# A shorter work share in every second long period of an attention and SwiGLU kernel's instruction order

## The chip, the core and the metric

The kernel runs on one core of a Trainium2 chip. The metric is the device time of one execution in microseconds. The core has five engines that run side by side, each through its own instructions in order: TensorE (PE; its weight loads, PEld, overlap its matmuls), VectorE (DVE), ScalarE (ACT), GpSimd (POOL) and SyncE (SP), whose queue issues most DMAs. They wait for one another through semaphores. Matmuls write PSUM banks, from which VectorE and ScalarE read.

## What is computed

`x` is 2048 × 512. One half of the kernel is softmax attention with 32 heads of 16, the other a SwiGLU block with 1792 inner columns; a gate per token mixes them.

```python
def _A_ref(x, wqkv, wo):
    ...
    scores = jnp.einsum("bhqd,bhkd->bhqk", q, k) * scale
    p = _softmax(scores, axis=-1)
    o = jnp.einsum("bhqk,bhkd->bhqd", p, v)
    return (lambda x, *d: x.transpose(*d))(o, 0, 2, 1, 3).reshape(B, S, D) @ wo

def _B_ref(x, w1, w3, w2):
    gate = jnp.einsum("bsd,df->bsf", x, w1)
    up = jnp.einsum("bsd,df->bsf", x, w3)
    h = _silu(gate) * up
    out = jnp.einsum("bsf,fd->bsd", h, w2)
    return out

g = _sigmoid((x * gate_w).sum(-1, keepdims=True))
return g * a + (1 - g) * b
```

## The kernel before

A prologue transposes and splits x, projects V and the first 128 columns of Q and K, and writes Q and K to device memory. Matrix products outside attention are made of three products of a high and a low half of each operand (fh, fl for weights, xH, xL for x; the names xH and xL are used again later for the halves of w2 and of the attention output).

Then one long loop, about 1280 us, mixes two streams on TensorE. Its order is a string, `order`, one letter per piece of TensorE work:

- **Q**: a unit of scores. There are 1024 units, 32 for each of 32 steps (a pair of heads and half of the queries). A unit is two matmuls, side by side in the two 64-row halves of the array, into a buffer S of two PSUM banks; there are two such buffers. ScalarE then takes the exp of the unit into one of eight buffers p (L795).
- **P**: the weighted sums with V (called PV below) of the two oldest units, four matmuls over the full array into `acc` (L779). After the sixteenth key tile `evac` copies `acc` to `u` on VectorE and stores it (L766, L773).
- **F**: a work slot. Each slot issues up to one matmul in each of two lanes, the two 64-row halves of the array, from a list of blocks: the remaining Q and K columns, gate and up products in chunks of 128 columns (L432), the products of h with w2 (L550), the first part of the output projection (L636, L643). A block of `length` slots runs first in one lane and then, at least GAP later, in the other; when both are done VectorE (and ScalarE) take it from its bank. The matmul of the second half waits for a small VectorE memset, `tick` (L752).

A period is eight Q with its F and P. In `one`, the long period, it is two scores and six slots, then a score and three slots five times, one last score and four P in a row. In `two`, the double, it is fifteen slots, and the four P stand in two groups of two with two scores between. The first part of the loop is long periods, the second doubles; the joint between them begins with `QQFFF`.

Other work is hung on the letters. At every Q, one or more items of `small` (pieces of the gate's sigmoid on VectorE), `loads` (loads of w2 rows and of pieces of h, each with a split into halves on GpSimd, L513 and L514) and `stages` (division by the softmax sums) are issued. `load_step` issues the Q and K rows of the next step, fourteen DMAs, when the count of units is 6 modulo 32. Weight splits (L328, L329) are issued a fixed number of units after their load. `load_w2` is added to `loads` when the last up block of a column block is done, so it follows the F stream; a step's loads follow the Q stream. SP takes all these DMAs in the order in which they are issued.

After the loop, `while feed()` empties the lanes, and the rest of the output projection is done with full-array matmuls (L96 to L98).

Of the kernel before, what the change touches and what calls it, by code (L numbers as in the profile page):

```python
# [33 lines left out]
def gated_mix_kernel(ctx: ExitStack, tc: tile.TileContext, x, wqkv, wo, w1, w3, w2, gate_w, out):  # L34
# [765 lines left out]


    NP = 8
    LONG, SHORT = 77, 51
    one = "QQFFFFFF" + "QFFF" * 5 + "QPPPP"
    two = "QFFF" * 5 + "QPPQQPP"
    order = one * LONG + "QQFFF" + two * (SHORT - 1) + "QFFF" * 4 + "QFQPPPP"
    free = list(range(NP))

    units = iter([(j, half, k, gq) for half in range(2) for j in range(NPAIR) for k in range(NT) for gq in range(2)])
# [112 lines left out]
```

## Time and profile before

| | us |
|---|---|
| median of 3 runs | 1403.82 |
| the three runs | 1403.82, 1403.74, 1717.74 |
| profiled execution, time | 1402.91 |
| profiled execution, span | 1401.1 |

The span runs from the first to the last instruction of the profiled execution; its time is 1.8 us longer. The granted TensorE clock is 1.000 over the span. In the rows below, a timeline row is: start, duration, engine, line, operation, output <- inputs, count of equal instructions merged, and in brackets the idle time before and what ended it. A row of the chain is: start, duration, engine, tile, line. A row of a group is: line, engine, operation, count, then busy time and the mean ns of one, then the idle time before. Ends of matmuls are modelled, so starts are compared. A TensorE row of 0.39 us whose successor starts 0.23 later is an overlapped pair.

### The profile page before, as it was taken

Reading aid. Unit: us, or ns where it says so; the run is one execution under the profiler, and the core shown is the slowest. Engines: PE = TensorE matmul, PEld = TensorE weight load, DVE = VectorE, ACT = ScalarE, POOL = GpSimd, SP = SyncE. Lnnn points to the kernel's source line nnn. Section 1 sums busy time; section 2 is a strip of 40 time slices with the busy share of each in tenths; the row PEclk is TensorE's granted clock in tenths of the full one; section 3 lists DMA queues with packets and bytes.
Section 4 is the critical chain, followed back from the end, with each engine's and each line's share of the span. In section 5 each row is a group of like instructions: output and inputs, shape, how many; then the busy total and the mean of one; then the engine's idle time right before and its main releaser. Section 6 shows DMA issues by size and latency. Waiting matters only on the chain.

```text
span 1401.1 us, 28802 instructions
## 1 busy us (share of the span) xinstructions
PE 1394.2 (100%) x11398; PEld 819.8 (59%) x11398; DVE 486.6 (35%) x1069; ACT 1032.8 (74%) x1153; POOL 321.1 (23%) x357
## 2 busy tenths in 40 slices
PE   9999999999999999999999999999999999999998
PEld 8866566565565565565565565555555555555556
DVE  5511111564545556555464654411111111110013
ACT  4457677777777777777777777788778878877880
POOL 6123433011011101110110117241233232133240
PEclk9999999999999999999999999999999999999999
DMA  7753564343223423223332236444443433355445
GB/s 205 174 121 97 135 135 112 74 112 77 50 54 84 114 55 84 62 67 96 69 77 70 78 80 169 97 99 98 106 96 89 109 102 81 63 127 116 89 136 178
DMA packets 112814, 141.44 MB, mean 101 GB/s; under 512 B 16416, under 2 KB 70944, under 8 KB 109600
## 3 DMA queue, kind: packets, MB, share of 16 engines
q1 hardware_dynamic: 110240, 135.32, 40.8%
q10 hardware_dynamic: 2432, 4.20, 0.9%
q8 instruction: 92, 1.51, 0.5%
q14 instruction: 50, 0.41, 0.1%
HBM read 90.70 MB, written 48.76 MB: 100 GB/s over the span
## 4 chain that ended last, share of the span: by engine, by line
PE 99%; ACT 0%; DVE 0%; issue 0%; DVEq 0%; ACTq 0%
PE acc L779 33%; PE f L432 27%; PE S L791 19%; PE f L550 11%; PE S L199 2%; PE f L96 1%; PE f L98 1%; PE f L97 1%; PE f L636 1%; ACT p L795 0%; PE acc L353 0%; PE f L165 0%; PE S L98 0%; PE S L97 0%; PE S L96 0%; PE S L165 0%
## 5 line engine op out<-in xcount | busy, mean ns | idle before, releaser
L795 ACT ACTIVATE p<-S 128x1024 f32<-128x1024 f32 x1024 | 967.4, 1026 | 298.9 <-PE S L791 289.7
L779 PE MATMUL acc<-p,V 128*17 128x512 f32 x4096 | 474.1, 594 | 0.0
L791 PE MATMUL S<-Qt,Kt 50*128 50x512 f32 x2048 | 402.7, 408 | 1.2 <-DVE V L415 0.7
L791 PEld LDWEIGHTS S<-Qt,Kt 50*128 50x128 f32 x2048 | 183.1, 184 | 186.3 <-ACT p L795 85.7
L779 PEld LDWEIGHTS acc<-p,V 128*17 128x17 f32 x4096 | 102.2, 97 | 272.2 <-issue 272.2
L463 DVE RECIPROCAL sg<-sg 128x64 f32<-128x64 f32 x448 | 209.1, 517 | 49.3 <-issue 47.3
L432 PE MATMUL f<-xL,fh 64*128 64x512 f32 x1088 | 218.0, 392 | 0.0
L432 PE MATMUL f<-xH,fl 64*128 64x512 f32 x1088 | 218.0, 392 | 0.0
L432 PE MATMUL f<-xH,fh 64*128 64x512 f32 x1088 | 217.1, 390 | 0.0
L432 PEld LDWEIGHTS f<-xH,fl 64*128 64x128 f32 x1088 | 104.9, 186 | 24.0 <-POOL fl L329 0.4
L432 PEld LDWEIGHTS f<-xL,fh 64*128 64x128 f32 x1088 | 105.1, 186 | 22.4
L432 PEld LDWEIGHTS f<-xH,fh 64*128 64x128 f32 x1088 | 104.3, 185 | 23.4
L752 DVE MEMSET tick<- 1x1 f32 x189 | 11.2, 59 | 272.8 <-PE f L550 155.0
L328 POOL CAST fh<-fr 128x512 fp32r<-128x512 f32 x34 | 21.6, 637 | 357.2 <-DMA fr<-in_B_w_dram 233.4
L455 DVE COPY gs<-f 128x512 f32<-128x512 f32 x56 | 38.7, 691 | 69.0 <-PE f L432 62.8
L550 PE MATMUL f<-xL,fh 64*128 64x512 f32 x208 | 61.8, 390 | 0.0
L550 PE MATMUL f<-xH,fl 64*128 64x512 f32 x208 | 60.8, 390 | 0.0
L550 PE MATMUL f<-xH,fh 64*128 64x512 f32 x208 | 59.9, 390 | 0.0
L550 PE MATMUL f<-xH,raw 64*128 64x512 f32 x192 | 57.4, 390 | 0.0
L461 DVE TENSOR_SCALAR sg<-sg 128x512 f32<-128x512 f32 x56 | 27.2, 485 | 81.7 <-ACT sg L460 79.6
L619 POOL TENSOR_TENSOR hx<-hx,gw 128x512 f32<-128x512 f32 x8 | 10.3, 1288 | 197.3 <-DMA gw<-r_d 186.7
L760 DVE COPY u<-acc 128x512 f32<-128x512 f32 x32 | 22.1, 692 | 96.1 <-PE acc L779 81.7
(230 smaller groups left out, 1281.4 us busy)
## 6 DMA issues: line engine op xcount, KB each, us to landing
Kt<-kH_d SPq DMA_DIRECT2D x128, 128.0 KB
h_d<-sg SPq DMA_DIRECT2D x56, 256.0 KB
sg<-h_d SPq DMA_DIRECT2D x43, 256.0 KB
fr<-in_B_w_dram SPq DMA_DIRECT2D x42, 256.0 KB
Qt<-qH_d SPq DMA_DIRECT2D x128, 64.0 KB
Kt<-kL_d SPq DMA_DIRECT2D x64, 128.0 KB
Qt<-qL_d SPq DMA_DIRECT2D x64, 64.0 KB
b_d<-y SPq DMA_DIRECT2D x16, 256.0 KB
```

What stands on the lines that cost most here:

```text
L96: nc.tensor.matmul(ps, sH, mH, start=first, stop=False)
L199: nc.tensor.matmul(ps[:, i, :], w[i][h][:, k, :], xs[b][:, k, :], start=n == 0, stop=n == len(order) - 1)
L328: nc.gpsimd.tensor_copy(hi, src)
L432: return nc.tensor.matmul(ps, w[i == 1][r, k, :], (xL if i == 2 else xH)[b][r, k, :], start=n == 0 and not second, stop=n == 3 * ND - 1 an ...
L455: nc.vector.tensor_copy(gs, ps)
L461: small.append(lambda: nc.vector.tensor_scalar(sg, sg, 1.0, None, op0=OP.add))
L463: small.append(lambda q=q: nc.vector.reciprocal(sg[:, q:q + 64], sg[:, q:q + 64]))
L550: ins = nc.tensor.matmul(ps, hs[t][q][i == 1][r, P * o:P * o + P], (w2L if i == 2 else w2H)[q][r, o, :], start=n == 0 and not second, stop ...
L760: nc.vector.tensor_copy(u, acc)
L779: nc.tensor.matmul(acc[r:r + DH + 1, :], V[:, k, 2 * j + h, :], p[:, h, :], start=k == 0, stop=k == NT - 1)
L791: nc.tensor.matmul(ps[:, h, :], Kt[i][r:r + 50, P * k:P * k + P], Qt[i][r:r + 50, t:t + 512], start=True, stop=True)
L795: nc.scalar.activation(p, ps, AF.Exp, scale=SCALE)
```

## The change

The long part had 77 periods `one`. It now has 37 pairs of `one` and `less`, and then nine more `one`, 83 periods in all. `less` is `one` with five slots instead of six between the second and the third score. The joint has four slots instead of three, and of the doubles 45 are left instead of 51 (the last one is written out with a different end).

```diff
-    LONG, SHORT = 77, 51
+    LONG, MID, SHORT = 37, 9, 45
     one = "QQFFFFFF" + "QFFF" * 5 + "QPPPP"
+    less = "QQFFFFF" + "QFFF" * 5 + "QPPPP"
     two = "QFFF" * 5 + "QPPQQPP"
-    order = one * LONG + "QQFFF" + two * (SHORT - 1) + "QFFF" * 4 + "QFQPPPP"
+    order = (one + less) * LONG + one * MID + "QQFFFF" + two * (SHORT - 1) + "QFFF" * 4 + "QFQPPPP"
```

Slots before: 77 × 21 + 3 + 50 × 15 + 13 = 2383. Slots after: 37 × 41 + 9 × 21 + 4 + 44 × 15 + 13 = 2383. Scores, PV and blocks are the same in number.

TensorE's order, second period, one piece of the difference (f is a bank of the work, S a score buffer):

```order
 L432 MATMUL f<-xL_158,fh_652 128x512
 L432 MATMUL f<-xL_158,fh_646 128x512
+L791 MATMUL S<-Qt_108,Kt_111 128x512 x2
 L432 MATMUL f<-xH_157,fh_652 128x512
 L432 MATMUL f<-xH_157,fh_646 128x512
-L791 MATMUL S<-Qt_108,Kt_111 128x512 x2
 L432 MATMUL f<-xH_157,fl_653 128x512
```

The third score of the period stands one slot (two matmuls) earlier.

SP's order where the work goes over from gate and up to the h products, before (`fr<-in_B_w` of 128x512 are rows of w2, `sg<-h_d` pieces of h, `d_d<-u` and `o_d<-u` the stores of `evac`, Qt, Kt and `m_d` the operands of a step):

```order
L512 DMA fr<-in_B_w_dram 128x512 x2
L512 DMA sg<-h_d 128x4x128
L482 DMA h_d<-sg 128x512
L512 DMA sg<-h_d 128x4x128 x2
L512 DMA sg<-h_d 128x2x128
L766 DMA d_d<-u 1x512 x4
L773 DMA o_d<-u 16x512 x4
L277 DMA Qt_109<-qH_d 16x1024
```

SP's order behind the same `evac`, at the same step, after the change:

```order
L512 DMA fr<-in_B_w_dram 128x512
L277 DMA Qt_109<-qH_d 16x1024
L277 DMA Qt_109<-qL_d 16x1024
L277 DMA Qt_109<-qH_d 16x1024 x2
L277 DMA Qt_109<-qL_d 16x1024
L277 DMA Qt_109<-qH_d 16x1024
L270 DMA Kt_112<-kH_d 16x2048 x2
L270 DMA Kt_112<-kL_d 16x2048
L270 DMA Kt_112<-kH_d 16x2048 x2
L270 DMA Kt_112<-kL_d 16x2048
L282 DMA Qt_109<-m_d 2x1024 x2
L512 DMA fr<-in_B_w_dram 128x512
```

The last two row blocks of w2 were ahead of the stores and of the step; now one is between them and the last is behind the step.

TensorE's order at the end of the loop, before:

```order
L779 MATMUL acc<-p_20915,V 17x512 x2
L779 MATMUL acc<-p_20925,V 17x512 x2
L779 MATMUL acc<-p_20930,V 17x512 x2
L96 MATMUL f<-xH_15791,raw 128x512
L97 MATMUL f<-xL_15792,raw 128x512
L98 MATMUL f<-xH_15791,raw 128x512
```

And after the change (`L643` is the last block of the output projection's first part, the one that is split between the lanes):

```order
L779 MATMUL acc<-p_20917,V 17x512 x2
L779 MATMUL acc<-p_20923,V 17x512 x2
L643 MATMUL f<-wo_19904,fl_20358 128x512
L643 MATMUL f<-wo_19904,fh_20357 128x512
L643 MATMUL f<-wo_17915,fh_20357 128x512
L643 MATMUL f<-wo_17915,fl_20358 128x512
L643 MATMUL f<-wo_17915,fh_20357 128x512
L96 MATMUL f<-xH_15867,raw 128x512
L97 MATMUL f<-xL_15868,raw 128x512
L98 MATMUL f<-xH_15867,raw 128x512
```

Five matmuls of that block now stand behind the last P, ahead of the tail. Within the loop 2370 slots hold two matmuls, 12 hold one and one is empty before; 2364 hold two and 19 hold one after.

## Prediction

> **What bounds the kernel now.** I read the busy times first, then the chain that ended last, then the timeline of single periods.
>
> ```profile
> PE 1394.2 (100%) x11398; PEld 819.8 (59%) x11398; DVE 486.6 (35%) x1069; ACT 1032.8 (74%) x1153; POOL 321.1 (23%) x357
> PE 99%; ACT 0%; DVE 0%; issue 0%; DVEq 0%; ACTq 0%
> L795 ACT ACTIVATE p<-S 128x1024 f32<-128x1024 f32 x1024 | 967.4, 1026 | 298.9 <-PE S L791 289.7
> L779 PE MATMUL acc<-p,V 128*17 128x512 f32 x4096 | 474.1, 594 | 0.0
> ```
>
> TensorE is never free and the chain is 99% TensorE, so a change that only reorders pays or gains through two things: extra TensorE time at switches, and TensorE waiting. ScalarE is the second busiest, and its idle time ends on scores (S), so it is the first engine TensorE could come to wait for. The chain gives the long period, by the starts of its weighted sums (PV, written acc, L779):
>
> ```profile
> 87.31 3.56 PE acc L779 x32
> 286.75 3.56 PE acc L779 x32
> 297.23 3.56 PE acc L779 x32
> 874.58 3.56 PE acc L779 x32
> ```
>
> From 87.31 to 874.58 lie 75 long periods: 787.27 / 75 = 10.497 us. Most take 10.50, some 10.48 (286.75 to 297.23). The doubles, from the timeline of TensorE, where a block of PV is half as long:
>
> ```profile
> 904.71 1.91 PE L779 MATMUL acc<-p,V 128*17 128x512 f32 x16
> 914.13 1.91 PE L779 MATMUL acc<-p,V 128*17 128x512 f32 x16
> 1102.46 1.91 PE L779 MATMUL acc<-p,V 128*17 128x512 f32 x16
> ```
>
> 914.13 to 1102.46 is 20 doubles of 9.417 us. A long period has 21 work slots and a double 15, with the same scores and PV. The timeline of one long period shows a slot's price and who is close behind:
>
> ```profile
> 300.71 0.73 PE L791 MATMUL S<-Qt,Kt 50*128 50x512 f32 x4
> 301.32 7.54 ACT L795 ACTIVATE p<-S 128x1024 f32<-128x1024 f32 x8 [2.45 <-PE S L791]
> 302.45 0.19 PEld L791 LDWEIGHTS S<-Qt,Kt 50*128 50x128 f32 x2
> 302.69 0.39 PE L791 MATMUL S<-Qt,Kt 50*128 50x512 f32 x2
> 302.92 0.40 PE L432 MATMUL f<-xH,fl 64*128 64x512 f32 x2
> 305.25 0.39 PE L432 MATMUL f<-xH,fh 64*128 64x512 f32 x2
> 307.65 3.63 PE L779 MATMUL acc<-p,V 128*17 128x512 f32 x32
> ```
>
> Starts on TensorE are 0.23 apart, so a slot costs 0.23 us. From the first two scores (300.71) to PV is 6.94. The third score reuses the S buffer that the first exp reads. That exp starts at 301.32 and, with the mean of 1.026, ends at 302.35; the score's weight load goes at 302.45. So only about 0.10 is free there, less than the slot that is taken out.
>
> **The change part by part.**
>
> *Six doubles become long periods.* Per pair 10.497 − 9.417 = 1.08, so 6 × 1.08 = +6.5 us. The six extra long periods bring 36 slots, and the joint between the two parts one more.
>
> *The joint.* It is `QQFFF` before and `QQFFFF` after. Its rows are also the best evidence for the next step:
>
> ```profile
> 888.57 0.73 PE L791 MATMUL S<-Qt,Kt 50*128 50x512 f32 x4
> 889.17 7.44 ACT L795 ACTIVATE p<-S 128x1024 f32<-128x1024 f32 x8 [2.45 <-PE S L791]
> 890.25 0.50 PE L791 MATMUL S<-Qt,Kt 50*128 50x512 f32 x2 [0.25 <-ACT p L795]
> 895.31 1.91 PE L779 MATMUL acc<-p,V 128*17 128x512 f32 x16
> ```
>
> With three slots ahead of the third score TensorE waits for the exp (0.25 shown), so a fourth slot there is hidden: 0. If the exp came earlier it would cost 0.23.
>
> *Thirty-seven periods lose a slot, 21 to 20.* The joint is such a period with two slots fewer still: three F stand before its third score where the short period has five, and all else up to PV is alike. From 888.57 to 895.31 is 6.74, against 6.94. Three slots (0.70) were taken out and 0.20 came back; the rest went into the wait for the exp. A short period, with one slot out (0.23), can't come below this floor, so it saves 0.20, or 0.18 where the long one took 10.48. Bounds: 0 (the wait eats the slot) and 0.23 (nothing waits). I take 0.19, near the joint's row: 37 × 0.19 = −7.0 us. The exps keep up: eight take 7.44 at the joint, (7.44 − 1.03)/7 = 0.92 or a little less each, against 0.93 for a score and its three slots.
>
> The Trainium skill ("ScalarE: Activation LUTs", section "What ACT_TABLE_LOAD costs") gives an activation with immediate scale and bias as 186 ns + 0.833 ns per element with 93 ns overlap, an estimate of 0.946 us per exp here. By that ScalarE would be slower than the scores and most of the slot would turn into waiting, a sum of about +7.7 (the slow rival below). The rows above, under 0.92 where the exps set the pace, are shorter; I go by them.
>
> *The stall at 820.9 goes.*
>
> ```profile
> 819.20 1.65 POOL L329 TENSOR_TENSOR fl<-fr,fh 128x512 fp32r<-128x512 f32 x1
> 820.51 0.39 PE L791 MATMUL S<-Qt,Kt 50*128 50x512 f32 x2
> 820.90 0.50 PE L432 MATMUL f<-xH,fl 64*128 64x512 f32 x2
> 821.23 0.39 PE L432 MATMUL f<-xL,fh 64*128 64x512 f32 x2
> ```
>
> The last chunk's weights were split (819.20 + 1.65 = 820.85) just when TensorE needed them: 820.90 instead of 820.74, and the next pair 0.33 behind it instead of 0.23, so 0.25 in all. After the change the work lags the scores by some 35 slots here, so the same split, which follows the scores, is several microseconds early: −0.25 (bounds −0.25 and 0). Nothing is late next there: the scores are paced as elsewhere.
>
> *Five matmuls spill past the end.* Slots are 2383 in both orders, but in the new one the two lanes fall out of step more often (19 slots of one matmul, against 12 and an empty one), and five matmuls of the last o_half block, one lane, come after the last PV.
>
> ```profile
> 1364.09 0.39 PE L643 MATMUL f<-wo,fh 64*128 64x512 f32 x1
> 1364.32 0.39 PE L643 MATMUL f<-wo,fl 64*128 64x512 f32 x1
> 1365.42 0.50 PE L791 MATMUL S<-Qt,Kt 50*128 50x512 f32 x2 [0.25 <-ACT p L795]
> 1388.44 0.69 DVE L886 TENSOR_TENSOR p<-fr,p 128x512 fp32r<-128x512 f32 x1 [0.78 <-ACT p L885]
> 1391.43 0.39 PE L96 MATMUL S<-wo,p 128*128 128x512 f32 x1
> ```
>
> One lane alone also takes 0.23 per matmul, so 5 × 0.23 = +1.15 us. TensorE carries the tail: its last operand is ready at 1389.13 and used at 1391.43, so that 2.3 hides nothing of the five. The last period's slots, fuller than before, cost 0, since the last score waits 0.25 for its exp in any case; without that cover +0.23. Lower bound of the spill 0, if the tail waited for data.
>
> *A load falls behind a step's operands.* The loads of w2 follow the work, load_step follows the scores. The work is now some 20 slots later there, so w2's last row block, which stood ahead of the evacuation and load_step, stands behind step 21's fourteen DMAs on SP's queue (Qt, Kt and m_d). Nothing on TensorE waits for those DMAs soon, but the h product of token tile 0 needs that row block. Prices, SP and GpSimd (POOL):
>
> ```profile
> 878.14 0.66 PE S L791 x4
> 878.92 1.12 SPq L766 DMA_DIRECT2D d_d<-u  x4
> 881.88 0.37 SPq L512 DMA_DIRECT2D fr<-in_B_w_dram  x1
> 884.62 0.61 POOL L513 CAST xH<-fr 128x512 fp32r<-128x512 f32 x1 [4.41 <-DMA fr<-in_B_w_dram]
> 885.32 1.29 POOL L514 TENSOR_TENSOR xL<-fr,xH 128x512 fp32r<-128x512 f32 x1
> 922.98 0.36 SPq L277 DMA_DIRECT2D Qt<-qH_d  x1
> 929.15 1.12 SPq L512 DMA_DIRECT2D sg<-h_d  x2
> 935.02 0.61 POOL L513 CAST fh<-sg 128x512 fp32r<-128x512 f32 x1 [12.09 <-DMA sg<-h_d]
> ```
>
> Let T be the first scores of the period that begins with unit 640 (878.14 is such a place). The stores start at T + 0.8 and the first w2 load goes at T + 3.7, as in these rows. The fourteen DMAs take 929.15 − 922.98 = 6.2, so the last w2 load goes near T + 10.4. A w2 load alone reaches GpSimd 2.7 later (881.88 to 884.62); a load right behind a step's fourteen, 5.9 later (929.15 to 935.02). The split adds 0.61 + 1.29 and a gap, 2.0. So the low half is ready between T + 15.1 and T + 18.3. TensorE wants it in the next period at the third slot after the fifth score: T + 10.5 + (305.25 − 300.71) = T + 15.0. The wait is 0.1 to 3.3; I take 2.2, nearer the load behind a step, because Kt's bytes have to drain first, but w2's rows are longer pieces than h_d's. No other work covers it: TensorE runs in order.
>
> *Sum:* 6.5 + 0 − 7.0 − 0.25 + 1.15 + 2.2 = +2.6. The profiled execution took 1402.91 (span 1401.1), so 1405.5; the median shown, 1403.82, lies 0.9 higher, so I give 1406.4.
>
> **The rivals.**
>
> *Forecast, 0.64:* as summed. With the w2 wait from 0.1 to 3.3 and the saving from 0.17 to 0.21 per short period, 1403.5 to 1408.3.
>
> *The load lands in time, 0.16:* w2's rows pass the Kt rows and the wait is 0. Then +0.4, 1404.2. For it: 2.7 alone. Against it: 5.9 behind a step. The Trainium skill ("DMA: Bandwidth & Descriptors", section "Anatomy of one DMA — SWDGE (gpsimd) path") fits 2.0 us plus the bytes at 436 GB/s, an estimate of 2.6 for 256 KB, for another issue path; it agrees with the load alone and says nothing against the backlog.
>
> *Nothing waits, faster, 0.06:* each short period saves the full 0.23 (−8.5) and the load is in time: 6.5 − 8.5 − 0.25 + 1.15 = −1.1, 1402.7. Against it: the 0.10 that is free, and the joint.
>
> *ScalarE sets the pace of short periods, slower, 0.11:* the last score of a period waits for the sixth exp, which hangs on the five exps before it at p each. At the joint p was 0.92 and PV came at 6.74; with a slower p it comes at 6.74 + 5 × (p − 0.92). At p = 0.95 that is 6.89, so a short period saves 0.05, 37 × 0.05 = 1.9, and the change is 6.5 − 1.9 − 0.25 + 1.15 + 2.2 = +7.7, 1411.5. It decides as soon as p passes the 0.93 that TensorE gives a score and its three slots. For it: the eight exps from 301.32 took 0.93 each. Against it: there they waited on scores; at the joint, where a score waited on an exp, they were faster.
>
> *Some other block finds its operand late, 0.03:* as at 820.90, but for microseconds; 2.5 to 9 more than the forecast, 1409 to 1415.
>
> **How the numbers follow.** The predicted time is the forecast's, 1406.4. The forecast's range and the second case (0.80 together) lie within 1403.0 to 1409.0, which also leaves a little for uneven long and double periods (10.48 to 10.50 and 9.41 to 9.42, some ±0.5 us in all). A gain or loss of 2%, about what a measurement of this kernel can tell from no change, is 28 us. The slow rival would need 0.76 lost in each of the 37 short periods to reach it, and the fast one has no source for 28. So faster 0.01, same 0.97, slower 0.02, the latter two for what none of these cases names.
>
> **What would show it.** Right: short periods of 10.28 to 10.31 us, third scores in them marked as waiting for ACT p L795 by a few hundredths to 0.2; 83 long-type starts, then doubles of 9.41; no gap of 0.15 at the last chunk's first slot; five L643 rows after the last PV; one gap of 0.1 to 3.3 us on TensorE ahead of L550, released by POOL xL L514, in the second period after unit 640. Wrong: short periods at 10.27 (nothing waits) or 10.45 to 10.50 (ScalarE paces); no gap at L550, or gaps at other blocks; a gap between PV and the tail's first matmuls.

## The result, and the profile after

| | us |
|---|---|
| median of 5 runs, after | 1419.09 (1417.5 to 1421.79) |
| median before | 1403.82 |
| ratio after / before | 1.011, 95% interval 1.0099 to 1.0121 |
| profiled execution, time / span | 1418.07 / 1416.2 |

The one execution of the kernel before that took 1717.74 us was in a slower state and is left out of the ratio.

The changed kernel is 1.1% slower: +15.3 us, where +2.6 was forecast; its 1419.09 lies beyond 1409.0, the end of the forecast's range.

From the page of the changed kernel: its busy times, its chain by engine, and three groups (last in a row stands the idle time just before them and what ended it):

```profile
PE 1401.6 (99%) x11398; PEld 822.7 (58%) x11398; DVE 483.8 (34%) x1069; ACT 1028.5 (73%) x1153; POOL 319.5 (23%) x357
...
PE 92%; issue 4%; POOL 2%; DMA 1%; SPq 1%; DVE 1%; DVEq 0%; POOLq 0%
...
L432 PE MATMUL f<-xH,fh 64*128 64x512 f32 x1088 | 222.6, 392 | 3.3 <-DVE tick L752 3.3
L432 PE MATMUL f<-xH,fl 64*128 64x512 f32 x1088 | 223.2, 392 | 2.2 <-DVE tick L752 2.2
...
L550 PE MATMUL f<-xH,fh 64*128 64x512 f32 x208 | 70.6, 391 | 2.0 <-POOL xH L513 2.0
```

The chain was 99% TensorE and is now 92%; SP, POOL and DMA have come into it. TensorE waits 3.3 + 2.2 us for ticks, the small memset of L752 that lets the second half of a block write the bank, and 2.0 us for the split of w2 at L513. The busy time of TensorE has grown by 7.4 us with the same 11398 matmuls, so it seems to have run slower somewhere, too.

Where the time went is read from the starts of the periods. I count them from 0, each from the weight load of its first score to the next such load. The changed kernel's timeline, weight loads of TensorE, period 5:

```profile
133.25 0.30 PEld L791 LDWEIGHTS S<-Qt,Kt 50*128 50x128 f32 x4 [0.85 <-issue]
...
147.74 0.30 PEld L791 LDWEIGHTS S<-Qt,Kt 50*128 50x128 f32 x4 [0.85 <-issue]
```

That is 14.49 us, where the other short periods take 10.33 (median of 37). Period 12, a long one, takes 13.86 instead of 10.49, period 81, long too, 15.16, and period 72 takes 10.97. These four hold 4.16 + 3.36 + 4.66 + 0.48 = 12.7 of the span's 15.1 us. The rest: +6.5 for six doubles that became long periods, −6.0 for the short periods, −0.3 for the stall that is gone, +1.4 in the tail, +0.8 ahead of the first score.

**Period 5.** The changed kernel's timeline (start, duration, engine, line, operation): SP's queue, DVE, then TensorE.

```profile
132.46 0.57 SPq L282 DMA_DIRECT2D Qt<-m_d  x2
133.86 0.34 SPq L187 DMA_DIRECT2D qL_d<-gs  x1
...
140.60 0.69 DVE L443 COPY gs<-f 128x512 f32<-128x512 f32 x1 [4.67 <-DMA qL_d<-gs]
141.23 0.06 DVE L752 MEMSET tick<- 1x1 f32 x1
...
138.77 0.39 PE L791 MATMUL S<-Qt,Kt 50*128 50x512 f32 x2
141.35 0.50 PE L432 MATMUL f<-xH,fl 64*128 64x512 f32 x2 [2.19 <-DVE tick L752]
...
142.49 5.32 PE L779 MATMUL acc<-p,V 128*17 128x512 f32 x32
```

A finished Q/K block is copied into a `gs` tile (L443), split, and stored (L187). There are two such tiles. The stores of an earlier block now stand on SP behind the fourteen DMAs of step 2 (the last two of them are the row at 132.46). The store of 133.86 lands only at 140.5, by the last update of its semaphore, so the next copy waits 4.67 us for its tile, and the tick behind it in DVE's order waits with it. TensorE's start comes 2.58 us after the one before it instead of 0.23. When this store was issued, the last four of the step's Kt loads, 128 KB each by the page's list of DMA issues, had not landed (they land from 134.8 to 137.9), nor had the 256 KB store ahead of it (139.1). In steps_late, an experiment below in which the step's DMAs go later, the same store lands 3.4 us after its issue and not 6.6.

**Period 12** has the same wait, and other DMAs stand ahead of the stores, the evacuation's d_d and o_d (changed kernel, timeline of SP, DVE and TensorE):

```profile
212.18 1.69 SPq L773 DMA_DIRECT2D o_d<-u  x4
213.97 1.51 SPq L187 DMA_DIRECT2D qH_d<-sg  x1
215.58 0.38 SPq L187 DMA_DIRECT2D qL_d<-gs  x1
...
219.03 0.69 DVE L443 COPY gs<-f 128x512 f32<-128x512 f32 x1 [5.49 <-DMA qL_d<-gs]
...
219.78 0.50 PE L432 MATMUL f<-xH,fh 64*128 64x512 f32 x2 [3.08 <-DVE tick L752]
```

In the kernel before, the stores of two more blocks went ahead of this evacuation (202.22 to 205.49, the evacuation from 207.15); now all stand behind it, and three blocks follow one another on the two tiles. No run moved these stores alone, so how much of the delay is the evacuation's and how much the closer blocks' stays open.

**Period 81** is the place that the prediction named (changed kernel, timeline of SP, POOL and TensorE):

```profile
934.11 0.36 SPq L512 DMA_DIRECT2D fr<-in_B_w_dram  x1
...
939.33 1.27 POOL L514 TENSOR_TENSOR xL<-fr,xH 128x512 fp32r<-128x512 f32 x1
...
939.31 0.49 PE L550 MATMUL f<-xH,fh 64*128 64x512 f32 x1 [1.98 <-POOL xH L513]
...
940.66 0.49 PE L550 MATMUL f<-xL,fh 64*128 64x512 f32 x1 [0.62 <-POOL xL L514]
```

The waits are 2.0 and 0.6, but the period lost 4.7; and in period 5 the PV that follows the wait takes 5.25 us to the next score (142.49 to 147.74) instead of 3.56. The windows of the changed kernel (stretch and its length, busy time and count of PE, PEld, DVE, ACT, POOL, then the granted TensorE clock, the DMA share and GB/s) show why:

```profile
130.40:141.40 11.00, 8.81 (x78) 4.92 (x70) 1.38 (x3) 7.02 (x8) 3.61 (x5) 1.00 0.94 172
141.40:147.70 6.30, 6.30 (x40) 1.77 (x40) 0.00 (x0) 1.02 (x1) 1.85 (x2) 0.73 0.55 166
...
219.80:227.00 7.20, 7.20 (x62) 3.38 (x64) 0.06 (x1) 3.41 (x4) 1.88 (x2) 1.00 0.71 172
...
940.00:952.00 12.00, 11.38 (x86) 6.57 (x86) 0.18 (x3) 6.19 (x7) 9.20 (x12) 0.86 0.31 89
```

After the waits of periods 5 and 81 the clock was halved for 3.41 us (0.5 × 3.41 / 6.3 = 0.27 missing in the second row, 0.5 × 3.41 / 12 = 0.14 in the last), which costs half of that, 1.7 us. After the longer wait of period 12 it was not. So there are two things to test: that the order on SP makes the waits, and what makes the clock fall.

### The profile page after: what moved, and what is told of

It is laid out like the page before. It is cut to its first block, busy times and chain, and to the rows that moved or that the text cites. A ratio compares the mean times of both kernels' runs of the same rounds, so it can differ in the third digit from the quotient of the medians.

```text
span 1416.2 us, 28801 instructions
## 1 busy us (share of the span) xinstructions
PE 1401.6 (99%) x11398; PEld 822.7 (58%) x11398; DVE 483.8 (34%) x1069; ACT 1028.5 (73%) x1153; POOL 319.5 (23%) x357
## 4 chain that ended last, share of the span: by engine, by line
PE 92%; issue 4%; POOL 2%; DMA 1%; SPq 1%; DVE 1%; DVEq 0%; POOLq 0%
PE acc L779 30%; PE f L432 24%; PE S L791 18%; PE f L550 11%; PE S L199 2%; PE f L96 1%; PE f L98 1%; PE f L97 1%; PE f L636 1%; POOL gs L445 1%; POOL sg L444 0%; DMA qH_d<-sg 0%; PE f L165 0%; SPq L277 0%; DMA fr<-in_B_w_dram 0%
## 5 line engine op out<-in xcount | busy, mean ns | idle before, releaser
L791 PE MATMUL S<-Qt,Kt 50*128 50x512 f32 x2048 | 411.5, 411 | 0.8 <-DVE V L415 0.7
L432 PE MATMUL f<-xH,fh 64*128 64x512 f32 x1088 | 222.6, 392 | 3.3 <-DVE tick L752 3.3
L432 PE MATMUL f<-xH,fl 64*128 64x512 f32 x1088 | 223.2, 392 | 2.2 <-DVE tick L752 2.2
L432 PE MATMUL f<-xL,fh 64*128 64x512 f32 x1088 | 222.6, 391 | 0.0
L432 PEld LDWEIGHTS f<-xH,fh 64*128 64x128 f32 x1088 | 109.1, 185 | 23.1 <-DVE tick L752 3.5
L432 PEld LDWEIGHTS f<-xH,fl 64*128 64x128 f32 x1088 | 109.6, 186 | 21.7 <-DVE tick L752 2.6
L432 PEld LDWEIGHTS f<-xL,fh 64*128 64x128 f32 x1088 | 109.2, 185 | 19.2
L752 DVE MEMSET tick<- 1x1 f32 x189 | 11.2, 59 | 272.5 <-PE f L550 153.1
L550 PE MATMUL f<-xH,fl 64*128 64x512 f32 x208 | 74.1, 390 | 0.0
L550 PE MATMUL f<-xL,fh 64*128 64x512 f32 x208 | 72.0, 391 | 0.6 <-POOL xL L514 0.6
L550 PE MATMUL f<-xH,fh 64*128 64x512 f32 x208 | 70.6, 391 | 2.0 <-POOL xH L513 2.0
L550 PE MATMUL f<-xH,raw 64*128 64x512 f32 x192 | 59.3, 391 | 0.0
```

The source lines that it names most:

```text
L432: return nc.tensor.matmul(ps, w[i == 1][r, k, :], (xL if i == 2 else xH)[b][r, k, :], start=n == 0 and not second, stop=n == 3 * ND - 1 an ...
L550: ins = nc.tensor.matmul(ps, hs[t][q][i == 1][r, P * o:P * o + P], (w2L if i == 2 else w2H)[q][r, o, :], start=n == 0 and not second, stop ...
L791: nc.tensor.matmul(ps[:, h, :], Kt[i][r:r + 50, P * k:P * k + P], Qt[i][r:r + 50, t:t + 512], start=True, stop=True)
```

## The experiments

All times stand beside the kernel before on the same chip: 1403.9 us for the first four, 1403.54 for the last three.

**steps_late: two steps later on SP**

```diff
-            if issued % 32 == 6 and step < 2 * NPAIR:
+            if issued % 32 == (12 if step in (2, 21) else 6) and step < 2 * NPAIR:
```

> The changed kernel, but the loads of steps 2 and 21 go to SP's queue six units later (issued % 32 == 12 for these two, 6 for the others), so that in period 5 the Q/K stores of L187 and in period 81 the last row of w2 stand ahead of the step's 14 DMAs again. Nothing else is moved, and period 12, where the stores stand behind the evacuation's, stays as it is. Theory (the time was lost to blocks that found their operand late because their DMA stood behind a step's on SP): periods 5 and 81 fall from 14.49 and 15.16 to the 10.33 of their kind, both halved stretches of the clock go with them, period 12 stays at 13.9; 1419.1 - 4.2 - 4.6 = 1410.3 us (1409 to 1411.5). Rival A (the clock falls because the stream of work is denser now, and the waits lie elsewhere): a halved stretch of 3.4 us is still somewhere, 1412 to 1414. Rival B (the transfers are late through their own load on the DMA engines, wherever the step stands): 1417 to 1420.

1411.92 us (1408.63 to 1412.27), ratio 1.0053 [1.0036, 1.007]: just above the theory's range and below rival A's, so the traces decide. In the trace of steps_late the stores of period 5 go ahead of the step again, and of TensorE's groups one wait for a tick is left (timeline of SP, then the group):

```profile
132.47 0.34 SPq L187 DMA_DIRECT2D qL_d<-gs  x1
...
140.67 0.38 SPq L277 DMA_DIRECT2D Qt<-qH_d  x1
```

```profile
L432 PE MATMUL f<-xH,fh 64*128 64x512 f32 x1088 | 222.9, 393 | 3.2 <-DVE tick L752 3.2
```

Periods 5 and 81 take 10.33 and 10.49, as the others of their kind (81 and 12 are long ones; the 10.33 expected of them was a slip). Rival B falls. But period 12, untouched, took 16.68 instead of 13.86: its wait is 2.96 now, and the clock was at half for 6.83 us behind it. Rival A had a fall of the clock left over, but for another reason: here the wait is one that the changed kernel has at the same place, and it halved the clock in this execution and not in that one. One of the four runs took 1408.63 at a mean clock of 0.999, the others 1411.74 to 1412.27 at 0.997.

**lo_raw: a third buffer for the stores**

```diff
-            lo = slot("gs", F32)
+            lo = slot("raw", F32)
```

> The changed kernel, but the low half of a Q/K block lies in a tile named raw, which has three buffers, and no longer in one named gs, which has two. The order on SP is untouched: in period 5 the stores still stand behind the step, in period 12 behind the evacuation's. Theory (the DVE copy of L443 waits for a buffer whose store has not landed, and the tick that TensorE needs stands behind that copy in DVE's order): with a third buffer the copy and the tick are in time, periods 5 and 12 fall from 14.49 and 13.86 to 10.33, with period 5's halved clock; period 81 stays at 15.2; 1419.1 - 4.2 - 3.4 = 1411.5 us (1410.5 to 1413). Rival (the wait only goes on to the next tile in the row, the high half sg with its two buffers, by way of POOL's queue, and from there to a later operand): less than half of it goes, 1416 to 1419.

1410.15 us (1409.84 to 1412.45), ratio 1.0047 [1.0031, 1.0064], a little below the theory's range. The stores still stand behind the step; periods 5 and 12 take 10.33 and 10.48. TensorE's groups in lo_raw's trace keep only the wait of period 81, and the copy in period 5 now waits for TensorE, not for a store (timeline of DVE):

```profile
L432 PE MATMUL f<-xH,fh 64*128 64x512 f32 x1088 | 222.8, 392 | 0.2 <-DVE tick L752 0.2
...
L550 PE MATMUL f<-xH,fh 64*128 64x512 f32 x208 | 70.6, 391 | 3.0 <-POOL xH L513 3.0
```

```profile
137.35 0.69 DVE L443 COPY raw<-f 128x512 f32<-128x512 f32 x1 [1.25 <-PE f L432]
```

So the path from late store to tile to copy to tick is shown: the order on SP was taken away in steps_late, the shortage of tiles here, and the last link, from copy to tick, stands in DVE's rows of period 5. The profiled execution's period 81 took 16.16 us, with 2.97 of wait and a halved stretch.

**both_mended: both edits**

> Both edits together: steps 2 and 21 six units later, and the low half in raw. Theory: periods 5, 12 and 81 all stand at 10.33, no stretch of halved clock is left before the end, and what remains of the change is the rest of the forecast's sum: 1419.1 - 4.2 - 3.4 - 4.6 = 1406.9 us (1405.5 to 1408), that is 3 us above the kernel before, of which 1.4 lie behind the last PV and 0.8 ahead of the first score. Rival (37 short periods cost in other places than the three, or the clock falls all the same): above 1409.

1406.37 us (1405.69 to 1407.24, ten runs), ratio 1.002 [1.001, 1.0029], as the theory had it. Periods 5, 12 and 81 take 10.34, 10.50 and 10.49. The chain of both_mended's page and its largest wait among L432 and L550:

```profile
PE 99%; DVE 0%; DMA 0%; ACT 0%; issue 0%; DVEq 0%
```

```profile
L432 PE MATMUL f<-xH,fh 64*128 64x512 f32 x1088 | 222.4, 392 | 0.2 <-DVE tick L752 0.2
```

The clock is at full through the whole span: its next fall is recorded at 1404.21, behind the last instruction (the span is 1404.0). Some 12.7 of the 15.3 us (1419.09 − 1406.37) are thus the three places. Against the kernel before, 2.5 us are left.

**before_early: the same wait put into the kernel before**

```diff
-            if issued % 32 == 6 and step < 2 * NPAIR:
+            if issued % 32 == (4 if step in (2, 21) else 6) and step < 2 * NPAIR:
```

> The kernel before with nothing of the change, but the load of step 2 goes to SP's queue two units earlier (issued % 32 == 4 for steps 2 and 21; step 21 has no load near it here), so that the Q/K stores of period 5 stand behind the step's 14 DMAs, as in the changed kernel. Theory (the order on SP alone makes the wait): period 5 rises from 10.50 to about 14.5, with a tick that comes 2 us late and a halved stretch of the clock behind it; 1403.8 + 4.0 = 1407.8 us, or 1406.0 if the wait comes and the clock stays. Rival (it needs the short periods, which leave less time between two blocks): period 5 stays at 10.5, 1403.8 us.

1407.8 us (1406.64 to 1408.87), ratio 1.0031 [1.0019, 1.0042]. In its trace the step's DMAs go from 126.27, ahead of the stores (timeline of SP, DVE and TensorE, and the window behind the wait):

```profile
133.24 0.34 SPq L187 DMA_DIRECT2D qL_d<-gs  x1
...
140.36 0.69 DVE L443 COPY gs<-f 128x512 f32<-128x512 f32 x1 [5.24 <-DMA qL_d<-gs]
...
141.10 0.50 PE L432 MATMUL f<-xH,fl 64*128 64x512 f32 x2 [3.04 <-DVE tick L752]
```

```profile
141.60:145.00 3.40, 3.40 (x20) 1.86 (x20) 0.06 (x1) 1.42 (x2) 1.40 (x2) 0.50 0.47 156
```

Two units of difference in when one step is issued, with no short period anywhere, cost 3.9 us by the medians; in the profiled execution period 5 took 15.34 instead of 10.50. The kernel before was that close to it.

**stalls: what a wait does to the clock**

```diff
-    REST, GAP = 9, 6
+    REST, GAP = 9, 6
+    DOSE = {20 + 5 * i: 12 + 2 * (3 * i % 7) for i in range(21)}
...
                     turn = nc.vector.memset(tick[:, 0:1], 0.0)
                     after(turn, ins)
+                    for _ in range(DOSE.get(t["id"], 0)):
+                        turn = nc.vector.memset(tick, 0.0)
```

> The kernel before with waits of measured length put in: behind the tick of 21 of its blocks, five blocks apart, DVE clears a row of 128 numbers 12 to 24 times, and the second half's first matmul waits for the last of them, so that TensorE stands still for some 0 to 4 us at places where no step's load and no evacuation is due. What is counted is the halved stretches of the clock behind them. Theory, from the records of the changed kernel and of steps_late, lo_raw and before_early: the clock goes by stretches of 3.41 us that follow one another without a gap from its first rise on, and a stretch in which TensorE was idle for about half (1.7 us or more) is followed by one at half speed, which costs up to 1.7 us beyond the wait. So no idle time under 1.7 us halves it, one between 1.7 and 3.4 us does or does not by how it lies across two stretches, and one above 3.5 us always does. Rival A: only a whole idle stretch of 3.4 us halves it (then nothing below 3.4 us does). Rival B: the halving belongs to the transfers of a step or of an evacuation nearby, and not to the idle time (then none of these waits, far from both, halves it). The time itself tells nothing: 1403.9 us plus the waits and 1.7 us for each halved stretch.

One execution, 1455.81 us. Twelve of the 21 places gave a wait of 0.8 us or more; at the other nine it was hidden. The granted clock first rises at 5.59 us of the span, and every later change in its records is a whole number of 3.413 us behind that, so the span can be laid out in stretches of that length. The idle time of TensorE is taken from the modelled end of the last matmul ahead to the start of the next:

```
idle from-to, us    total  in each stretch it touches  clock behind it
201.57-202.38       0.81   0.81                        full
235.07-237.59       2.52   2.52                        half for 3.41
331.13-334.84       3.71   2.14, 1.57                  half for 6.83
370.12-371.42       1.30   0.70, 0.60                  full
394.87-397.65       2.78   2.78                        half for 3.41
491.37-495.34       3.97   2.32, 1.64                  half for 6.83
530.41-532.71       2.30   0.84, 1.46                  full
565.74-569.01       3.27   3.05, 0.22                  half for 3.41
685.48-687.76       2.29   2.29                        half for 3.41
721.97-725.96       3.99   0.42, 3.41, 0.15            half for 3.41
760.35-762.14       1.79   1.79                        half for 3.41
855.97-858.96       2.99   2.95, 0.03                  half for 3.41
```

The clearest pair, by stalls' timeline of TensorE and the windows of the stretches in question:

```profile
532.71 0.50 PE L432 MATMUL f<-xH,fl 64*128 64x512 f32 x2 [2.30 <-DVE tick L756]
...
687.76 0.49 PE L432 MATMUL f<-xH,fl 64*128 64x512 f32 x1 [2.29 <-DVE tick L756]
```

```profile
688.20:691.60 3.40, 3.40 (x20) 2.70 (x18) 3.01 (x6) 1.39 (x2) 0.00 (x0) 0.51 0.02 5
...
531.20:534.60 3.40, 1.90 (x16) 1.59 (x17) 2.90 (x12) 0.94 (x2) 0.00 (x0) 1.00 0.00 0
```

Two waits of 2.3 us: one lay inside one stretch and was followed by 3.4 us at half clock, the other lay across two and cost nothing more. Rival A falls, since waits of 1.79 to 3.27 us are followed by a halved stretch, and rival B, since the DMA engines are all but idle here (a share of 0.02). A stretch with 1.79 us or more of idle time is followed by half clock, one with 1.46 or less is not, and one at half clock that is itself idle for 1.57 or 1.64 is followed by another. At half clock less is enough: in steps_late's period 12 the halved stretch has only 0.61 us of idle time and a second one follows, while 0.22, 0.15 and 0.03 here are followed by full clock. The mixed cases of the changed kernel lie between, 1.75 us in period 12 without a fall and 1.69 in period 81 with one; modelled ends don't resolve these. The waits add up to 31.7 us and eleven stretches at 1.7 to 18.8, less 1.8 for idle time inside them: 48.7 of the 52.3 us. The other 3.6 lie in the same twelve periods, up to 0.6 at each wait beyond its idle time and the halved clock: with the clock at full behind it, the wait of 0.81 made its period 1.30 longer, the one of 1.30 1.94 and the one of 2.30 2.71.

**six_back: six periods get their slot back, on both_mended**

```diff
-    order = (one + less) * LONG + one * MID + "QQFFFF" + ...
+    order = (one + less) * (LONG - 6) + one * (MID + 12) + "QQFFFF" + ...
```

> both_mended with 31 short periods instead of 37 (six have their 21st slot back), so that the feed-forward work runs out ahead of the last PV and no L643 matmul is left behind it. Theory: what stands behind the last PV falls by the 1.4 us that the five spilled matmuls and the change of tiles cost, and six periods of 10.33 become 10.49: 1406.4 - 1.4 + 1.0 = 1406.0 us (1405.3 to 1406.8), the way from the last PV to the first L96 back at 3.56 us. Rival (the tail's 1.4 us are something else, such as the last evacuation): 1407.4 us and 4.92 us on that way.

1406.15 us (1405.34 to 1407.1), ratio 1.0018 [1.0009, 1.0028]. From the last PV to L96, first in the changed kernel and then in six_back (timeline of TensorE):

```profile
1379.51 3.63 PE L779 MATMUL acc<-p,V 128*17 128x512 f32 x32
...
1383.40 0.62 PE L643 MATMUL f<-wo,fh 64*128 64x512 f32 x2
...
1384.43 0.50 PE L96 MATMUL f<-xH,raw 128*128 128x512 f32 x1
```

```profile
1369.46 3.63 PE L779 MATMUL acc<-p,V 128*17 128x512 f32 x32
1373.02 0.50 PE L96 MATMUL f<-xH,raw 128*128 128x512 f32 x1
```

4.92 us against 3.56: the tail's 1.36 are the five spilled matmuls. The slots that remove them cost almost as much elsewhere. Six periods are 0.17 longer, 1.0 together, and period 81 is late once more: it takes 11.19 instead of 10.49, since a piece of h was split too late (six_back, timeline of TensorE):

```profile
933.89 0.50 PE L550 MATMUL f<-xH,fr 64*128 64x512 f32 x1 [0.41 <-POOL fr L514]
```

Period 72, late by 0.5 in both_mended, is back at 10.50. By the times alone, 0.2 us with wide overlap, the two kernels can't be told apart.

**slot_m1: the slot missing in another place, on both_mended**

```diff
-    less = "QQFFFFF" + "QFFF" * 5 + "QPPPP"
+    less = "QQFFFFFF" + "QFF" + "QFFF" * 4 + "QPPPP"
```

> both_mended with the slot of a short period missing behind its third score, not ahead of it (QQFFFFFF QFF QFFF... in place of QQFFFFF QFFF QFFF...). Theory (in a short period the third score waits for the first exp, which swallows a part of what the missing slot saves): with the six slots back ahead of the third score the whole slot is saved, a short period takes 10.29 to 10.31 instead of 10.33, and 37 of them give about 1 us: 1405.4 us (1404.6 to 1406.2). Rival (ScalarE's exps set the pace through the whole period, the fourth to eighth score included): 10.33 as before or longer, 1406.4 us or more.

1406.47 us (1405.82 to 1407.44), ratio 1.0021 [1.0011, 1.003]: no gain, short periods 10.34. The theory of the wait at the third score alone falls. Weight loads of TensorE in one short period, first score, third score, first load of PV, in both_mended:

```profile
403.33 0.30 PEld L791 LDWEIGHTS S<-Qt,Kt 50*128 50x128 f32 x4 [0.85 <-issue]
405.01 0.19 PEld L791 LDWEIGHTS S<-Qt,Kt 50*128 50x128 f32 x2 [0.22 <-ACT p L795]
...
410.09 0.13 PEld L779 LDWEIGHTS acc<-p,V 128*17 128x17 f32 x8 [0.31 <-issue]
```

and in slot_m1, first score, fourth score, first load of PV:

```profile
403.98 0.30 PEld L791 LDWEIGHTS S<-Qt,Kt 50*128 50x128 f32 x4 [0.85 <-issue]
406.58 0.19 PEld L791 LDWEIGHTS S<-Qt,Kt 50*128 50x128 f32 x2 [0.19 <-ACT p L795]
...
410.76 0.13 PEld L779 LDWEIGHTS acc<-p,V 128*17 128x17 f32 x8 [0.29 <-issue]
```

In both the score behind the missing slot waits for an exp, and PV comes 6.76 and 6.78 us after the first score. From that score on every score's load goes 0.05 us after the end of the exp that frees its buffer, two units earlier (median over the periods 20 to 44), where the long period has 0.1. So ScalarE's exps set the pace of the rest of the period, wherever the slot is missing.

## Why the prediction was wrong

*Six doubles become long periods, +6.5:* right; long 10.497 and double 9.413 in both_mended (medians), 6 × 1.08 = 6.5. *The joint, 0:* right, 8.59 us in both kernels. *The stall at 820.9:* gone, as forecast, but a tick came 0.2 us late one pair of periods on, and period 72 took 0.5 more, in steps_late, lo_raw and both_mended too. No run was made to remove that one.

*Thirty-seven periods lose a slot, −7.0:* the floor was right (6.76 for 6.74) and its size a little off: 37 short periods are 6.3 us shorter than 37 long ones in steps_late (382.0 against 37 × 10.497), 0.17 each. The rival of ScalarE's pace has its mechanism, not its price: the exps come 0.90 to 0.92 us apart, below the 0.93 from which it would have decided.

*Five matmuls spill, +1.15:* right in kind, 1.36 measured, since two of the five are followed at 0.33 us and not at 0.23.

*A load falls behind a step's operands, +2.2:* this is the step that failed, twice. Its mechanism and its own wait were right (1.98 + 0.62 on TensorE, forecast 0.1 to 3.3): the low half was ready at 940.60, 18.0 us after the first scores of the period of unit 640 (922.60), within the bounds of 15.1 and 18.3. But it looked through SP's queue for loads of w2 only. The same shift, work that falls behind the scores by a slot in every second period, put the Q/K stores of two other places behind a step and an evacuation, and a store releases a tile just as a load fills one. The prediction had this as the rival "Some other block finds its operand late", at 0.03 and with no place. That is what happened, at two places, and it cost 4.2 and 3.4 us; even that rival's range, 1409 to 1415, was passed. For period 5 it could be seen beforehand, in the kernel before (timeline of SP):

```profile
131.00 0.34 SPq L187 DMA_DIRECT2D qL_d<-gs  x1
131.43 0.38 SPq L277 DMA_DIRECT2D Qt<-qH_d  x1
```

The store and the step's first DMA are neighbours on the queue, with nothing between them. The 0.43 us between the two rows is no reserve of time: the queue keeps the program's order, and a block that ends a slot or two later in that order falls behind all fourteen.

And it priced the wait alone. Of the 4.66 us of period 81 and the 4.16 of period 5, 1.7 each are the halved clock behind the wait, of which the trace of before, with no wait of TensorE over 0.3 us in its loop, showed nothing.

*Sum:* without the three places the change costs 2.5 us by both_mended. The prediction's sum without its load is +0.4. The difference: 0.7 to 1.2 in the short periods (the larger figure with the third buffer, whose sharing disturbs a few periods by 0.1 to 0.25), 0.5 in period 72, 0.2 in the tail, and the rest small.

No version here beats the kernel before. A slot costs 1.08 / 6 = 0.18 us where it goes from the doubles to a new long period and saves 0.17 where it is taken from a long one, so the trade has next to nothing to win even when no block is late; the other way, a 22nd slot in a long period, was not tried.

## What to carry to other kernels

Where two streams share a DMA queue and one is shifted against the other, list everything that stands on the queue near each burst, in the order of the program and not by its times, stores that release buffers as much as loads, and follow each to the engine that waits behind it. Price a wait of TensorE of about 1.7 us or more with the clock behind it. And before rows are traded between two kinds of period, set the price of a slot in the one against its worth in the other: here they were all but equal, so only the risk was left.

## What the runs showed of the hardware

In every trace here the granted clock changes in steps of 3.413 us from its first record on, and a full-speed stretch of that length in which TensorE was idle for about half or more (1.79 us and up; 1.46 is not enough) is followed by one at half speed. So about the same wait may cost 1.7 us more, or 3.4, or nothing, by where it falls. That fits the spread of the runs, too: the five of the changed kernel lie within 4.3 us, the two fastest at a mean clock of 0.998 and the others at 0.996 and 0.995, where a halved stretch takes 0.0012 off the mean (0.5 × 3.413 / 1416). The Trainium skill ("TensorE: Matmul & The Clock Gate", section "Part 1: The HAM clock gate (the "warmup" mystery)") describes such a free-running window of 3413 ns, and the records agree to the nanosecond. It gives about one idle window of 3.4 us as what lowers the clock; here 1.79 us of idle time in one stretch was enough, and the measurement decides.

The time of the first score goes with the same clock. Its first record, at full speed, stands at 4.47 us of the span in before and at 7.06 in steps_late; in steps_late matmuls start 0.21 us apart ahead of it and 0.11 behind it, so this is where the clock rises. In the nine profiled executions, whose kernels have the same code ahead of the first score, that score comes at 80.15 us where the record stands at 4.47, at 80.29 for 5.05, at 80.94 for 6.40 and at 81.33 for 7.06, in order throughout. So 0.8 of the 15.1 us between the two profiled spans goes with the start of the clock and not with the change.
